# Weaving the attention of each batch by hand into the feed-forward of the batch before it, with 1 KB load runs, 32x32 transposes on VectorE and column-tiled projections

## The chip, the cores and the metric

One core of a Trainium2 chip. The metric is the device time of one execution in microseconds (us). Executions of one kernel agree within about 1%. The profiled span is 1.7 to 1.8 us shorter than the time of the same execution, so sums of profile stretches are compared with spans, and times with times.

Engine names as the profile has them: PE is the matmul side of TensorE, PEld its weight loads, DVE is VectorE, ACT is ScalarE, POOL is GpSimd, SP the engine that only issues transfers here. PSUM is the memory that the matmuls write and the other engines read (the tiles with ps in their names); a copy out of it is an eviction. A column tile is a matmul with 32 weight columns, which fills 32 of the 128 PSUM partitions (`128*32` in the profile). An fp32 matmul shows as two records, which I call passes.

## The reference, cut to what matters

```python
# q, k, v: (4 batches, 4 heads, 1088 tokens, 32), fp32;  S1, S2: (8, 32)
def phi(x):
    a = einsum('rd,bhsd->bhsr', S1, x)
    b = einsum('rd,bhsd->bhsr', S2, x)
    return einsum('bhsi,bhsj->bhsij', a, b).reshape(..., 64)   # outer product
q_p, k_p = phi(q), phi(k)
kv  = einsum('bhsf,bhsd->bhfd', k_p, v)
z   = sum(k_p, over tokens)
att = einsum('bhsf,bhfd->bhsd', q_p, kv) / (einsum('bhsf,bhf->bhs', q_p, z) + 1e-6)
x   = att as (4352 tokens, 128)
out = (maximum(x @ w_gate, 0) * (x @ w_val)) @ w_out           # 128 -> 1536 -> 128
```

The attention needs all keys of a batch before its first query. The feed-forward (FFN) needs only the x of its own tokens. It is worked off in chunks of 512 tokens (8.5 chunks), each with 12 slices of 128 hidden units. I call one slice of one chunk a slot.

## The kernel before

One loop over batches does the attention, 128 tokens at a time. The FFN is a second loop, behind the last batch.

```python
for b in range(B):
    load_qkv(k4, k, nc.sync); load_qkv(q4, q, nc.sync); load_qkv(v4, v, nc.gpsimd)  # 128-byte runs
    for ci in range(NCH):                                    # K half
        nc.tensor.transpose(tr_ps, k4[:, ci], ident)         # fp32, on PE
        nc.vector.tensor_copy(out=tr_sb, in_=tr_ps)
        nc.tensor.matmul(ab_ps, tr_sb, s_bd)                 # 64 projected columns
        nc.scalar.copy(out=ab_sb, in_=ab_ps)
        ...                                                  # zbig, outer product on POOL, kv
    ...
    for ci in range(NCH):                                    # Q half: the same, 96 columns
        ...                                                  # then transposes, num / den, x transposed

for (c0, cs) in TCH:                                         # the FFN
    for j in range(NJ):
        nc.tensor.matmul(g_ps, wg_sb[:, j], xT[:, c0:c0+cs])
        nc.scalar.activation(out=g_sb, in_=g_ps, func=Relu)
        nc.tensor.matmul(v_ps, wv_sb[:, j], xT[:, c0:c0+cs])
        nc.vector.tensor_tensor(out=ht[:, j], in0=g_sb, in1=v_ps, op=mult)
    for j in range(NJ):
        nc.tensor.matmul(ot_ps, wo_sb[:, j], ht[:, j], start=(j==0), stop=(j==NJ-1))
    ...                                                      # transpose back, store
```

A scheduler decides the final order of the instructions on each engine.

Of the kernel before, what the change touches and what calls it, by code (L numbers as in the profile page):

```python
# [8 lines left out]
FP32 = mybir.dt.float32  # L10
BF16 = mybir.dt.bfloat16
FP16 = mybir.dt.float16
ALU = mybir.AluOpType
ACTF = mybir.ActivationFunctionType
XSCALE = 1.0 / 16.0


@with_exitstack
def kernel(
# [12 lines left out]
    nc = tc.nc  # L32
# [5 lines left out]
    NTOK = B * S  # L38
# [4 lines left out]
    SC = 128  # L43
    NCH = (S + SC - 1) // SC
    csz = [min(SC, S - i * SC) for i in range(NCH)]
    NFULL = S // SC
    CLAST = S - NFULL * SC
    HR = H * R

    const = ctx.enter_context(tc.tile_pool(name="const", bufs=1))  # L50
    xpool = ctx.enter_context(tc.tile_pool(name="xpool", bufs=1))
    a_in = ctx.enter_context(tc.tile_pool(name="a_in", bufs=2))
    a_tr = ctx.enter_context(tc.tile_pool(name="a_tr", bufs=5))
    a_ab = ctx.enter_context(tc.tile_pool(name="a_ab", bufs=5))
    a_kp = ctx.enter_context(tc.tile_pool(name="a_kp", bufs=5))
    a_qpt = ctx.enter_context(tc.tile_pool(name="a_qpt", bufs=5))
    a_sm = ctx.enter_context(tc.tile_pool(name="a_sm", bufs=6))
    a_pb = ctx.enter_context(tc.tile_pool(name="a_pb", bufs=2))
    f_h = ctx.enter_context(tc.tile_pool(name="f_h", bufs=2))
    f_g = ctx.enter_context(tc.tile_pool(name="f_g", bufs=4))  # L60
    f_o = ctx.enter_context(tc.tile_pool(name="f_o", bufs=4))


    ident = const.tile([128, 128], FP32)
    make_identity(nc, ident)
    ident16 = const.tile([128, 128], FP16)
    make_identity(nc, ident16)

    s_bd = const.tile([HD, 2 * HR], FP32)
    nc.vector.memset(s_bd, 0.0)  # L70
    for h in range(H):
        nc.scalar.dma_start(out=s_bd[h * D:(h + 1) * D, h * R:(h + 1) * R],
                            in_=S1.transpose([1, 0]))
        nc.scalar.dma_start(out=s_bd[h * D:(h + 1) * D, HR + h * R:HR + (h + 1) * R],
                            in_=S2.transpose([1, 0]))

    s1f = const.tile([HR, HD], FP32)
    nc.vector.memset(s1f, 0.0)
    for h in range(H):
        nc.scalar.dma_start(out=s1f[h * R:(h + 1) * R, h * D:(h + 1) * D], in_=S1)  # L80

    wg_sb = const.tile([DM, NJ, 128], FP16)
    nc.gpsimd.dma_start(out=wg_sb, in_=moe_w_gate.rearrange("m (j f) -> m j f", j=NJ))
    wv_sb = const.tile([DM, NJ, 128], FP16)
    nc.gpsimd.dma_start(out=wv_sb, in_=moe_w_val.rearrange("m (j f) -> m j f", j=NJ))
    wo_sb = const.tile([128, NJ, DM], FP16)
    nc.gpsimd.dma_start(out=wo_sb, in_=moe_w_out.rearrange("(j f) m -> f j m", f=128))

    xT = xpool.tile([HD, NTOK], FP16)

    with tc.tile_pool(name="ps_tr", bufs=2, space=bass.MemoryType.PSUM) as ps_tr, \
         tc.tile_pool(name="ps_xt", bufs=1, space=bass.MemoryType.PSUM) as ps_xt, \
         tc.tile_pool(name="ps_ab", bufs=1, space=bass.MemoryType.PSUM) as ps_ab, \
         tc.tile_pool(name="ps_kv0", bufs=1, space=bass.MemoryType.PSUM) as ps_kv0, \
         tc.tile_pool(name="ps_kv1", bufs=1, space=bass.MemoryType.PSUM) as ps_kv1, \
         tc.tile_pool(name="ps_zb", bufs=1, space=bass.MemoryType.PSUM) as ps_zb, \
         tc.tile_pool(name="ps_nd", bufs=1, space=bass.MemoryType.PSUM) as ps_nd:
        ab2_ps = ps_ab.tile([SC, 2, 96], FP32, name="ab2_ps")
        ndq2_ps = ps_nd.tile([SC, 512], FP32, name="ndq2_ps")
        xtsz_ps = ps_xt.tile([HD, 96], FP32, name="xtsz_ps")  # L100

        for b in range(B):
            q4 = a_in.tile([SC, NCH, H, D], FP32, name="q4")
            k4 = a_in.tile([SC, NCH, H, D], FP32, name="k4")
            v4 = a_in.tile([SC, NCH, H, D], FP16, name="v4")

            def load_qkv(dst, src, eng):
                for h in range(H):
                    eng.dma_start(
                        out=dst[:, 0:NFULL, h],  # L110
                        in_=src[b, h, 0:NFULL * SC, :].rearrange("(c p) d -> p c d", p=SC),
                    )
                eng.dma_start(
                    out=dst[:CLAST, NFULL],
                    in_=src[b, :, NFULL * SC:, :].transpose([1, 0, 2]),
                )

            load_qkv(k4, k, nc.sync)
            load_qkv(q4, q, nc.sync)
            load_qkv(v4, v, nc.gpsimd)  # L120

            kv_ps = [ps_kv0.tile([128, 2 * D], FP32, name="kv0_ps"),
                     ps_kv1.tile([128, 2 * D], FP32, name="kv1_ps")]
            zbig_ps = ps_zb.tile([HR, HR], FP32, name="zbig_ps")
            kv_bd = a_pb.tile([128, 2, F], FP16, name="kv_bd")
            s_bd_ext = a_pb.tile([HD, 3 * HR], FP32, name="s_bd_ext")
            zbig_sb = a_pb.tile([HR, HR], FP32, name="zbig_sb")

            nc.gpsimd.tensor_copy(out=s_bd_ext[:, 0:2 * HR], in_=s_bd)

            for ci in range(NCH):
                c = csz[ci]

                tr_ps = ps_tr.tile([HD, SC], FP32, name="tr_ps")
                nc.tensor.transpose(tr_ps[:, :c], k4[:c, ci].rearrange("s h d -> s (h d)"), ident[:c, :c])  # L135
                tr_sb = a_tr.tile([HD, SC], FP32, name="tr_sb")
                nc.vector.tensor_copy(out=tr_sb[:, :c], in_=tr_ps[:, :c])  # L137

                ab_ps = ab2_ps[:, ci % 2]
                nc.tensor.matmul(ab_ps[:c, 0:2 * HR], tr_sb[:, :c], s_bd, start=True, stop=True)  # L140
                ab_sb = a_ab.tile([SC, 96], FP32, name="ab_sb")
                nc.scalar.copy(out=ab_sb[:c, 0:2 * HR], in_=ab_ps[:c, 0:2 * HR])  # L142

                nc.tensor.matmul(  # L144
                    zbig_ps,
                    ab_sb[:c, 0:HR],
                    ab_sb[:c, HR:2 * HR],
                    start=(ci == 0), stop=(ci == NCH - 1),
                )

                kp = a_kp.tile([SC, H, R, R], FP16, name="kp")
                a_bc = ab_sb[:c, 0:HR].rearrange("s (h i) -> s h i", h=H)[:, :, :, None].to_broadcast([c, H, R, R])
                b_bc = ab_sb[:c, HR:2 * HR].rearrange("s (h j) -> s h j", h=H)[:, :, None, :].to_broadcast([c, H, R, R])
                nc.gpsimd.tensor_tensor(out=kp[:c], in0=a_bc, in1=b_bc, op=ALU.mult)  # L154

                for p in range(2):
                    kp_pair = kp[:c, 2 * p:2 * p + 2].rearrange("s h i j -> s (h i j)")
                    nc.tensor.matmul(  # L158
                        kv_ps[p],
                        kp_pair,  # L160
                        v4[:c, ci, 2 * p:2 * p + 2].rearrange("s h d -> s (h d)"),
                        start=(ci == 0), stop=(ci == NCH - 1),
                    )

            nc.scalar.copy(out=zbig_sb, in_=zbig_ps)
            nc.gpsimd.memset(kv_bd, 0.0)
            for p in range(2):
                nc.scalar.mul(out=kv_bd[0:F, p, 0:D], in_=kv_ps[p][0:F, 0:D], mul=XSCALE)
                nc.scalar.mul(out=kv_bd[F:128, p, D:2 * D], in_=kv_ps[p][F:128, D:2 * D], mul=XSCALE)

            sz_ps = xtsz_ps[:, 64:96]
            nc.tensor.matmul(sz_ps, s1f, zbig_sb, start=True, stop=True)
            nc.gpsimd.memset(s_bd_ext[:, 2 * HR:], 0.0)
            for h in range(H):
                nc.scalar.copy(out=s_bd_ext[h * D:(h + 1) * D, 2 * HR + h * R:2 * HR + (h + 1) * R],  # L175
                               in_=sz_ps[h * D:(h + 1) * D, h * R:(h + 1) * R])

            for ci in range(NCH):
                c = csz[ci]
                s0 = ci * SC  # L180

                tr_ps = ps_tr.tile([HD, SC], FP32, name="tr_ps")
                nc.tensor.transpose(tr_ps[:, :c], q4[:c, ci].rearrange("s h d -> s (h d)"), ident[:c, :c])  # L183
                tr_sb = a_tr.tile([HD, SC], FP32, name="tr_sb")
                nc.scalar.copy(out=tr_sb[:, :c], in_=tr_ps[:, :c])

                ab_ps = ab2_ps[:, ci % 2]
                nc.tensor.matmul(ab_ps[:c], tr_sb[:, :c], s_bd_ext, start=True, stop=True)  # L188
# [120 lines left out]
```

## Time and profile before

| | before |
|---|---|
| time, median of 3 runs | 224.61 us (223.93 to 225.66) |
| profiled span | 223.3 us |
| start of the dense FFN (first value matmul) | 144.18 us; the prediction reads about 143.5 |
| one batch of attention | 29.4 us |
| one FFN chunk | 8.5 us |

The page's first part gives busy time and its share of the span, its second cuts the span in 40 slices (the prediction shows those), and its third counts the packets of the transfers:

```profile
span 223.3 us, 3087 instructions
...
PE 179.1 (80%) x906; PEld 105.7 (47%) x906; DVE 106.2 (48%) x290; ACT 103.2 (46%) x307; POOL 82.1 (37%) x187
...
DMA packets 61776, 9.18 MB, mean 41 GB/s; under 512 B 57152, under 2 KB 61504, under 8 KB 61760
```

PE at 80% looks nearly full, but it is an average over two phases with different limits.

### The profile page before, as it was taken

The page shows a single profiled execution, that of the slowest core. Times are in us where ns is not written, and L with a number is a line of the kernel's source. Part 1 is how long each engine was busy: PE and PEld are TensorE (multiplying, and loading weights), DVE is VectorE, ACT ScalarE, POOL GpSimd, SP SyncE. Part 2 cuts the span into 40 slices and gives each one's busy share as a digit, 9 for nine tenths or more (in the row PEclk, how much of TensorE's full clock was granted, in tenths as well). Part 3 has the DMA queues.
Part 4 walks back from the last instruction along what each step waited for, and adds up shares of the span by engine and source line. Part 5 has one row for each costly group of instructions (what it writes and reads, how often), then busy time and mean ns, then how long its engine had stood idle before and what let it go on. Part 6 is the DMA issues. An engine that isn't in the chain of part 4 may idle for free.

```text
span 223.3 us, 3087 instructions
## 1 busy us (share of the span) xinstructions
PE 179.1 (80%) x906; PEld 105.7 (47%) x906; DVE 106.2 (48%) x290; ACT 103.2 (46%) x307; POOL 82.1 (37%) x187
## 2 busy tenths in 40 slices
PE   0018999659949989689997795599999999999992
PEld 0005666437727667366674552234444444444460
DVE  0002003333114431224422154369998989989981
ACT  0021243112433213332234362158898988988981
POOL 8402578997378853158632385000000000000000
PEclk9999999999999999999999999559999999999998
DMA  7999989765494100000000000000110110110110
GB/s 95 156 125 135 156 107 84 72 23 44 72 52 72 28 0 0 3 0 1 0 1 3 0 0 1 0 0 3 47 48 0 47 51 0 47 42 6 50 47 23
DMA packets 61776, 9.18 MB, mean 41 GB/s; under 512 B 57152, under 2 KB 61504, under 8 KB 61760
## 3 DMA queue, kind: packets, MB, share of 16 engines
q1 hardware_dynamic: 39952, 6.69, 17.8%
q0 software_dynamic: 19568, 2.30, 17.0%
q10 hardware_dynamic: 2240, 0.01, 0.7%
q8 instruction: 7, 0.11, 0.2%
q14 instruction: 9, 0.07, 0.1%
HBM read 9.06 MB, written 2.23 MB: 51 GB/s over the span
## 4 chain that ended last, share of the span: by engine, by line
PE 60%; POOL 18%; DMA 7%; issue 5%; DVE 4%; ACT 4%; SPq 0%; ACTq 0%; POOLq 0%
PE v_ps L255 12%; PE ot_ps L260 10%; PE g_ps L250 10%; POOL qp L195 8%; PE ab_ps L140 7%; DMA k<-in_k_dram 4%; PE zbig_ps L144 4%; POOL den L223 3%; POOL bw L215 3%; PE tr_ps L183 3%; PE kv_ps L158 2%; DMA s_bd<-in_S_dram 2%; PE xtsz_ps L236 2%; PE ndq_ps L211 2%; PE ab_ps L188 2%
## 5 line engine op out<-in xcount | busy, mean ns | idle before, releaser
L256 DVE TENSOR_TENSOR ht<-g_sb,v_ps 128x512 f16<-128x512 f16 (+1 forms) x108 | 67.3, 656 | 8.1 <-PE v_ps L255 4.0
L252 ACT ACTIVATE g_sb<-g_ps 128x512 f16<-128x512 f32 (+1 forms) x108 | 59.1, 583 | 11.5 <-PE g_ps L250 7.9
L255 PE MATMUL v_ps<-xT,wv_sb 128*128 128x512 f16 (+1 forms) x108 | 40.7, 379 | 0.8 <-DVE ht L256 0.4
L250 PE MATMUL g_ps<-xT,wg_sb 128*128 128x512 f16 (+1 forms) x108 | 40.9, 382 | 0.0
L260 PE MATMUL ot_ps<-ht,wo_sb 128*128 128x512 f16 (+1 forms) x108 | 39.8, 374 | 0.2 <-DVE ht L256 0.2
L154 POOL TENSOR_TENSOR kp<-ab_sb 128x256 f16<-128x256 f32 (+1 forms) x36 | 22.2, 623 | 23.8 <-ACT ab_sb L142 20.6
L135 PE MATMUL tr_ps<-ident,k 128*128 128x128 f32 (+1 forms) x36 | 14.7, 435 | 17.8 <-DMA k<-in_k_dram 14.2
L188 PE MATMUL ab_ps<-s_bd_ext,tr_sb 128*128 128x96 f32 (+1 forms) x72 | 25.3, 455 | 4.5 <-ACT s_bd_ext L175 2.6
L195 POOL TENSOR_TENSOR qp<-ab_sb 128x256 f16<-128x256 f32 (+1 forms) x36 | 22.5, 625 | 13.1 <-ACT ab_sb L190 12.3
L142 ACT COPY ab_sb<-ab_ps 128x64 f32<-128x64 f32 (+1 forms) x36 | 7.6, 211 | 41.0 <-PE ab_ps L140 31.8
L140 PE MATMUL ab_ps<-s_bd,tr_sb 128*128 128x64 f32 (+1 forms) x72 | 23.5, 431 | 2.3 <-DMA s_bd<-in_S_dram 2.3
L188 PEld LDWEIGHTS ab_ps<-s_bd_ext,tr_sb 128*128 128x128 f32 (+1 forms) x72 | 17.1, 298 | 9.6 <-ACT ab_sb L190 5.4
L137 DVE COPY tr_sb<-tr_ps 128x128 f32<-128x128 f32 (+1 forms) x36 | 9.6, 275 | 25.4 <-PE tr_ps L135 21.9
L222 DVE TENSOR_REDUCE den<-bw 128x4 f32<-128x32 f32 (+1 forms) x36 | 6.6, 184 | 30.6 <-POOL bw L215 30.3
L190 ACT COPY ab_sb<-ab_ps 128x96 f32<-128x96 f32 (+1 forms) x36 | 8.6, 238 | 25.7 <-PE ab_ps L188 22.4
L140 PEld LDWEIGHTS ab_ps<-s_bd,tr_sb 128*128 128x128 f32 (+1 forms) x72 | 17.5, 305 | 4.7 <-issue 3.1
L208 DVE COPY qpt<-ndq_ps 128x256 f16<-128x256 f16 (+1 forms) x36 | 10.0, 277 | 17.8 <-PE ndq_ps L202 17.2
L135 PEld LDWEIGHTS tr_ps<-ident,k 128*128 128x128 f32 (+1 forms) x36 | 8.0, 229 | 20.9 <-issue 14.4
L250 PEld LDWEIGHTS <-wg_sb 128*128 128x128 f16 x108 | 11.1, 103 | 13.2 <-issue 4.7
L260 PEld LDWEIGHTS <-wo_sb 128*128 128x128 f16 x108 | 10.6, 98 | 14.1 <-issue 3.8
L255 PEld LDWEIGHTS <-wv_sb 128*128 128x128 f16 x108 | 10.7, 99 | 12.6 <-issue 2.9
L237 ACT COPY xT<-xtsz_ps 128x128 f16<-128x128 f16 (+1 forms) x36 | 9.4, 261 | 14.8 <-PE xtsz_ps L236 14.7
(44 smaller groups left out, 207.5 us busy)
## 6 DMA issues: line engine op xcount, KB each, us to landing
k<-in_k_dram SPq DMA_DIRECT2D x16, 128.0 KB, 3.5
q<-in_q_dram SPq DMA_DIRECT2D x16, 128.0 KB, 4.6
out_dram<-o_sb SPq DMA_DIRECT2D x8, 256.0 KB, 2.3
v<-in_v_dram POOLq DMA_DIRECT2D x16, 64.0 KB, 3.4
wg_sb<-in_moe_w_gate_dram POOLq DMA_DIRECT2D x1, 384.0 KB, 5.9
wv_sb<-in_moe_w_val_dram POOLq DMA_DIRECT2D x1, 384.0 KB, 7.5
wo_sb<-in_moe_w_out_dram POOLq DMA_DIRECT2D x1, 384.0 KB, 11.0
s_bd<-in_S_dram ACTq DMA_DIRECT2D x8, 1.0 KB, 5.6
```

What stands on the lines that cost most here:

```text
L135: nc.tensor.transpose(tr_ps[:, :c], k4[:c, ci].rearrange("s h d -> s (h d)"), ident[:c, :c])
L137: nc.vector.tensor_copy(out=tr_sb[:, :c], in_=tr_ps[:, :c])
L140: nc.tensor.matmul(ab_ps[:c, 0:2 * HR], tr_sb[:, :c], s_bd, start=True, stop=True)
L154: nc.gpsimd.tensor_tensor(out=kp[:c], in0=a_bc, in1=b_bc, op=ALU.mult)
L188: nc.tensor.matmul(ab_ps[:c], tr_sb[:, :c], s_bd_ext, start=True, stop=True)
L195: nc.gpsimd.tensor_tensor(out=qp[:c], in0=a_bc, in1=b_bc, op=ALU.mult)
L208: nc.vector.tensor_copy(out=qpt[:, :, :c], in_=qpt_ps[:, :, :c])
L250: nc.tensor.matmul(g_ps[:, :cs], wg_sb[:, j], xT[:, c0:c0 + cs], start=True, stop=True)
L252: nc.scalar.activation(out=g_sb[:, :cs], in_=g_ps[:, :cs], func=ACTF.Relu)
L255: nc.tensor.matmul(v_ps[:, :cs], wv_sb[:, j], xT[:, c0:c0 + cs], start=True, stop=True)
L256: nc.vector.tensor_tensor(out=ht[:, j, :cs], in0=g_sb[:, :cs], in1=v_ps[:, :cs], op=ALU.mult)
L260: nc.tensor.matmul(ot_ps[:, :cs], wo_sb[:, j], ht[:, j, :cs], start=(j == 0), stop=(j == NJ - 1))
```

## The change

Its intent is to fill the half-idle engines of each phase with the work of the other. Batch 0 runs its attention alone. From then on the attention of batch b is issued, slot by slot, between the FFN slots of batch b-1, by an explicit plan and with the scheduler off. K and Q come in 1 KB runs instead of 128-byte ones. Their transposes are 32x32-block transposes on VectorE instead of PE transposes with evictions. The projections use four column tiles of 32 columns each, and q is divided by the denominator before its outer product. The core of the diff, with cuts marked:

```diff
+    if MANUAL:
+        ctx.enter_context(tc.manual_schedule())
 ...
-                    eng.dma_start(out=dst[:, 0:NFULL, h],
-                        in_=src[b, h, 0:NFULL * SC, :].rearrange("(c p) d -> p c d", p=SC))
+            engs[h % len(engs)].dma_start(
+                out=dst[h * D:(h + 1) * D, 0:32].rearrange("t (g c) d -> t g (c d)", g=4),
+                in_=src[b, h, 0:SM, :].rearrange("(g t c) d -> t g (c d)", g=4, t=32))
+        for g in range(2):                                   # the last 64 tokens, 128-byte runs
+            engs[g % len(engs)].dma_start(out=dst[:, 32 + g], in_=src[b, :, SM + 32 * g:SM + 32 * g + 32, :])
 ...
-                nc.tensor.transpose(tr_ps[:, :c], q4[:c, ci].rearrange("s h d -> s (h d)"), ident[:c, :c])
-                nc.scalar.copy(out=tr_sb[:, :c], in_=tr_ps[:, :c])
-                nc.tensor.matmul(ab_ps[:c], tr_sb[:, :c], s_bd_ext, start=True, stop=True)
-                nc.scalar.copy(out=ab_sb[:c], in_=ab_ps[:c])
+        nc.vector.transpose(out=qT[b][:, a * 32:e * 32], in_=q4[b][:, a:e].rearrange("p c d -> p (c d)"))
+        for s in range(3):                                   # sketch 1, sketch 2, denominator
+            for g in range(4):                               # column tile
+                nc.tensor.matmul(ps[32 * g:32 * g + 32, s * 128:(s + 1) * 128],
+                                 s_bd[:, s] if s < 2 else w_s[b], qT[b][:, c_cols(g, 4 * i, 4 * i + 4)])
+        nc.vector.transpose(out=ab[0:n], in_=st["qab", key][0:n, 0:384])
 ...
+    for b in range(1, B):
+        base = 2 * NJ * b                                    # first FFN slot of batch b
+        plan_k(b, base - 25)                                 # all this lies in slots of batch b-1
+        plan_q((b, 0), base - 9)
+        plan_q((b, 1), base - 5)
+    plan_q("rest", 2 * NJ * (B - 1) + 3)                     # the last 64 queries of all batches
+    for n in range(NSLOT):
+        at(n, ffn_gv, n)                                     # gate matmul, ReLU, value matmul of slot n
+        at(n + 0.9, ffn_mul, n)
+        at(n + lag, ffn_out, n)
+    for _, _, fn, a in sorted(table, key=lambda x: x[:2]):
+        fn(*a)
```

## The prediction

> **What bounds the kernel now.** I read the page's slices first, then the table by stage, then the chain, waits and timelines.
>
> ```profile
> PE   0018999659949989689997795599999999999992
> PEld 0005666437727667366674552234444444444460
> DVE  0002003333114431224422154369998989989981
> ACT  0021243112433213332234362158898988988981
> POOL 8402578997378853158632385000000000000000
> PEclk9999999999999999999999999559999999999998
> ```
>
> Two phases, hardly overlapped: POOL, which only attention uses, goes silent where DVE and ACT become full. The table by stretches (us, then busy us of each engine) takes one attention batch and one FFN chunk of 512 tokens:
>
> ```profile
> 79.28:108.64 29.36, 25.63 (x138) 18.12 (x138) 9.32 (x46) 9.29 (x45) 15.31 (x38) 1.00 0.00 1
> 187.50:196.00 8.50, 8.50 (x41) 3.70 (x40) 7.83 (x13) 7.49 (x15) 0.00 (x0) 1.00 0.11 31
> ```
>
> A batch takes 29.4 us (from the K phase of batch 2 to that of batch 3), and in it DVE and ACT are busy 9.3 us each: room for FFN work. An FFN chunk takes 8.5 us with PE, DVE and ACT all nearly full. The FFN starts at about 143.5 us, so 64% of the span is attention. In that phase the chain of waits jumps between engines:
>
> ```profile
> 97.76 0.62 POOL qp L195
> 99.03 0.59 POOL qp L195
> 100.25 0.58 POOL qp L195
> ```
>
> This is the Q half: one outer product each 1.2 us with its small POOL companions between. The first 17 us compute nothing, since K and the 4-byte-run S tables must land:
>
> ```profile
> 1.84 9.90 DMA k<-in_k_dram
> 11.76 5.04 DMA s_bd<-in_S_dram
> ```
>
> For the unit costs I read starts in the timelines, not durations, because matmul durations overlap: first four rows of the cold FFN start, then three of the steady FFN.
>
> ```profile
> 147.20 0.63 PE L260 MATMUL ot_ps<-ht,wo_sb 128*128 128x512 f16 x1
> 147.62 0.63 PE L250 MATMUL g_ps<-xT,wg_sb 128*128 128x512 f16 x1
> ...
> 187.35 0.38 PE L260 MATMUL ot_ps<-ht,wo_sb 128*128 128x512 f16 x1
> 187.56 0.38 PE L255 MATMUL v_ps<-xT,wv_sb 128*128 128x512 f16 x1
> 187.78 0.38 PE L250 MATMUL g_ps<-xT,wg_sb 128*128 128x512 f16 x1
> ```
>
> A 128x512 fp16 matmul costs 0.215 us of PE warm and 0.43 cold. Read alike, smallest start-to-start: the FFN multiply 0.605 us on DVE (256 columns 0.338, so 0.072 + 1.04 ns a column), the ReLU 0.476 on ACT (256: 0.264, so 0.052 + 0.83 ns a column), the POOL outer product of 256 elements 0.57 (of 32: 0.193, so 1.7 ns an element, 1.0 us for 512), an fp16 transpose on PE 0.055.
>
> **What the Trainium skill says.**
> "TensorE: Matmul & The Clock Gate", Part 1: the PE clock is halved until a window of about 3.4 us was busy. The trace agrees: 143.5 to 150.3 us, 6.8 us, ran at 0.5. In attention the record says 1.00, but most fp16 transposes started 0.107 us apart and not 0.055, so I take attention as mostly cold.
> "TensorEngine Tiling (Array Packing)", Key Properties: column tiles work independently, and a change of tiling mode drains the engine. Nothing here uses several column tiles at once. The drain shows: the two passes of the 32-column L144 start 0.075 us apart, the 128-column matmul behind them 0.17 us later.
> "VectorE: DVE Perf Modes", The three transpose paths: DVE transposes only within 32x32 blocks. No row here has one; I take 1 element a cycle like the other DVE work.
> "DMA: Bandwidth & Descriptors", Why small descriptors are slow: a fixed cost per packet. The trace agrees in kind: 57152 of 61776 packets are under 512 B, and loads ran at 125 GB/s in the first 17 us.
>
> **The change part by part.**
> *FFN arithmetic*: unchanged, 8.5 chunks. PE per chunk: 36 x 0.215 + 4 x 0.055 = 7.96 us (8.5 measured, so 6% bubbles).
>
> *Removed*: PE transposes of Q and K and their evictions, the ACT and DVE evictions of the projections, the x transposes; q is divided by the denominator before the outer product, so the numerator comes out transposed already.
>
> *Added on DVE, per batch*: 32x32 transposes of K and Q, 2 x (2 x 384 + 320 columns) = 2.7 us; of the projections 256 + 320 + 2 x 384 columns, 1.7 us; denominators and small copies about 1.2 us. Sum 5.6. Two chunks of FFN are 24 x 0.605 = 14.5, so DVE needs 20.1 us per batch.
>
> *ACT per batch*: 28 x 0.476 for ReLU and outputs, 2 evictions of 1024 columns at 0.90 and 2 of 512: 16.1 us. *POOL*: K 4 x 1.0 + 0.57, Q 4 x 1.0, smaller products about 1.5, DMA issue 1.6: 12 us. Neither bounds.
>
> *PE per batch*: two chunks 15.9 us; 18 kv matmuls at 0.05, 9 zbig at about 0.18 with their mode switches, 16 transposes, 4 x 0.215, sz: 4.7 us together. The disputed term is the fp32 projections: 80 passes of 128 moving columns and 16 of 32. From the cold spacings of the old projections (64 columns 0.268, 96 columns 0.321) a pass streams 1.67 ns a column cold, on top of a weight load that is not hidden; zbig (32 weights, 32 columns, 0.075) leaves 0.022 for a 32-column load. So 128 columns cost about 0.235 cold, 0.118 warm, and the batch 80 x 0.118 + 16 x 0.038 = 10.0 us if tiles do not overlap. With perfect fourfold overlap it would be 2.6, but about 0.046 per pass was the fastest issue seen, so 96 passes cannot go below 4.4. Each fp32 matmul has two passes on the same tile, which must follow each other, so I expect only the second pass of one tile to overlap with the first of the next: about 6.5 us.
> Sum 15.9 + 4.7 + 6.5 = 27.1 us per batch against 20.1 on DVE: PE bounds. But the load is uneven: a slot (1/24 of a batch) with a DVE transpose costs DVE about 1.07 us and PE 0.65, one with a Q projection PE over 2 us. With two PSUM buffers for gate and value only part evens out; taking the larger engine slot by slot gives 32, smoothing gives some back, so 28.
>
> *Prologue.* K goes first in 1 KB runs. Six issues at 0.57 us from 0.7, then a landing: K at about 6.3 us. Then three transposes 1.4, K projections cold 5, their transposes and outer products to about 15.5, kv and z to 18.5, two Q projections cold 3.6 each, outer products, transposes, evictions, numerators; the in-order PE does both halves of batch 0 before the first gate matmul. FFN start at about 30 us, against 143.5.
>
> *End.* The last 2.5 chunks host only the 256 remaining query rows: 2 x 8.5 + 3 + 4.4, then 4.3 us as before from the last ot to the stored result.
>
> *Sum*: 30 + 3 (cold first window or two of the FFN, as in the clock record now) + 3 x 28 + 28.7 = 145.7. I say 145.
>
> **The rivals.**
> A: column tiles overlap almost perfectly. Then a batch needs 15.9 + 4.7 + 4.4 = 25 us of PE, the prologue is some 3 us shorter, and DVE's uneven slots come next: 27 + 2 + 75 + 28.7 = about 133. For: the intent, and the skill; against: two passes on one tile.
> B: no overlap. 30.6 us per batch plus the uneven slots gives 32, the prologue grows by 4: 34 + 3 + 96 + 28.7 = 162. For: in the trace no fp32 weight load hides behind its own matmuls.
> C: woven in-order waits replace the old phase. One late qp or xT on the PE queue holds up gate and value, then DVE and ACT run dry. For: the old chain has many short waits, and the projections, transposes, numerators and outputs share two PSUM buffers. Against: the plan puts one to three slots, about 1 to 3 us, between producer and consumer, and a 512-element POOL product takes 1.0 us in 1.5 slots. If it costs 2 us more per batch: 151.
> D: loads still bound. Late weights would delay the FFN start. Weights, K, Q and V of batch 0 are about 3.8 MB to read, which at 125 to 180 GB/s takes 21 to 30 us; it could bind near 30, but only wo comes late and longer runs help.
>
> **Range and chances.** The main spread is the batch period, 25 to 32 us, counted three times (133 to 162 with the prologue's part); the prologue adds some 4 us either way. So 131 to 161. Even a period of 50 us would only give 211, below the 224.6 now, so slower is very unlikely: faster 0.97, same 0.02, slower 0.01.
>
> **What would show it right or wrong.** Right: POOL busy in tenths until about two thirds of the span; first gate matmul at 26 to 34 us; K landed by 7 us; gate and value spread at 24 slots per 25 to 32 us with PE over 90% and DVE about 70%; granted clock 1.0 after the first FFN microseconds; the last 2.5 chunks at 8.5 us. The start-to-start of the projection passes tells 0.118 (no overlap) from 0.07 (half) and 0.046 (issue-bound). Wrong: DVE above 90% in the woven part (a transpose then costs more than 0.47 us per 384 columns), the chain running through POOL or ACT there, PE at half clock again, or a wait on wg or wv at the FFN start.

## More of the kernel before

The costliest groups carry, after the bar, the engine's idle time just before them and what ended it:

```profile
L256 DVE TENSOR_TENSOR ht<-g_sb,v_ps 128x512 f16<-128x512 f16 (+1 forms) x108 | 67.3, 656 | 8.1 <-PE v_ps L255 4.0
L252 ACT ACTIVATE g_sb<-g_ps 128x512 f16<-128x512 f32 (+1 forms) x108 | 59.1, 583 | 11.5 <-PE g_ps L250 7.9
```

In the FFN before, VectorE and ScalarE hardly wait: 8.1 us of idle for 108 multiplies.

## The result, and the profile after

| | before | after |
|---|---|---|
| time, median of 4 runs | 224.90 us (223.93 to 225.66) | 164.75 us (164.23 to 165.39) |
| profiled span | 223.3 us | 163.4 us |
| packets under 512 B, of all | 57152 of 61776 | 5840 of 13535 |

The ratio is 0.7319 (95% interval 0.7286 to 0.7352). Ratios here are the mean time of one kernel's runs over that of the other's runs of the same rounds, so not quite the ratio of the medians quoted. Executions over 1.5% slower than the fastest of the same kernel are left out of the means. The kernel takes 27% less time, as the direction of the prediction said, and the result is correct. But 164.75 us lies above the range of 131 to 161.

The page of the changed kernel, first and second part and packets:

```profile
span 163.4 us, 2891 instructions
...
PE 122.2 (75%) x1038; PEld 61.1 (37%) x1038; DVE 100.2 (61%) x213; ACT 83.2 (51%) x146; POOL 51.1 (31%) x75
...
PE   0025884579997987779978885999887777999960
...
DVE  4313927415966678548648883786677546788740
...
POOL 8401614601940166156105625240176016000000
```

The phases are gone: POOL works until slice 34 of 40, and DVE is at 3 to 9 tenths beside it. But in the woven middle PE is mostly at 7 to 9 tenths, with one slice at 5, not "over 90%". The table by stages (start:end and length in us, busy us with instruction counts of PE, PEld, DVE, ACT and POOL, then clock, transfer share and GB/s) shows the prologue, the three woven batches, and the tail chunk by chunk:

```profile
0.00:34.66 34.66, 15.10 (x155) 9.65 (x155) 14.41 (x46) 4.10 (x5) 13.32 (x28) 1.00 0.88 148
34.66:63.66 29.00, 26.39 (x222) 12.46 (x221) 20.85 (x42) 16.96 (x29) 11.78 (x15) 1.00 0.12 20
...
94.88:126.10 31.22, 26.57 (x234) 13.05 (x234) 21.41 (x43) 19.00 (x32) 10.73 (x14) 1.00 0.05 17
126.10:141.10 15.00, 11.68 (x112) 5.44 (x112) 8.20 (x16) 9.53 (x17) 3.21 (x5) 1.00 0.05 19
141.10:150.40 9.30, 9.04 (x43) 3.77 (x41) 7.96 (x13) 8.35 (x16) 0.00 (x0) 1.00 0.09 31
```

Three things stand out against the prediction. The FFN starts at 34.66 us, not 30. A woven batch takes 31.22 us, not 28. And a chunk with no attention beside it (141.10 to 150.40) takes 9.30 us, where the kernel before needed 8.5 with the same instructions. No engine is full in a woven batch: DVE is busy 21.4 of 31.2 us, ACT 19.0 and POOL 10.7. PE's busy figure of 26.6 uses modelled ends and counts its pipelined matmuls long.

I put the excess together from the trace, against the predicted sum of 145.7, all in spans. The FFN start is 4.7 us late. From the first value matmul (35.09, 0.4 us after the gate) to the value matmul that opens the last two and a half chunks (126.32) it is 91.2 us, where I had 3 + 3 x 28 = 87, so 4.2 more. The tail from there to 163.43 is 37.1 us instead of 28.7, so 8.4 more. 4.7 + 0.4 + 4.2 + 8.4 = 17.7 us, which is 163.4 less 145.7.

**The prologue.** The chain that ended last, from the start (start us, length us, what):

```profile
2.90 0.74 SPq L82
3.69 9.44 DMA k<-in_k_dram
13.22 0.52 DVE kT L181
...
32.79 1.02 ACT qpt L343
```

The last piece of K is issued at 3.69 us and takes 9.44 us to land, although it has only 16 KB (part of this it stands behind the earlier pieces, for alone with Q and V it took 4.97 us in e2). Where the prediction has K at 6.3 us, the third K transpose starts at 13.22.

**The gate and the value.** In the waits view (what an engine waited for, us in total, times, longest) the two largest that touch the FFN are these:

```profile
ACT g_sb L377 <- PE g_ps L375: 39.4, 57, 2.4
...
DVE ht L386 <- ACT g_sb L377: 35.0, 45, 5.6
```

The multiply waits 35.0 us in 45 waits for the ReLU. In the kernel before, all idle time in front of the multiply was 8.1 us. A timeline of the chunk without attention (start us, length us, engine, line, operation) shows the pattern:

```profile
145.62 1.99 DVE L386 TENSOR_TENSOR ht<-g_sb,v_ps 128x512 f16<-128x512 f16 x3 [0.28 <-PE g_ps L375]
...
145.88 0.38 PE L375 MATMUL g_ps<-xT,wg_sb 128*128 128x512 f16 x1
146.37 0.38 PE L379 MATMUL v_ps<-xT,wv_sb 128*128 128x512 f16 x1
...
146.80 0.38 PE L375 MATMUL g_ps<-xT,wg_sb 128*128 128x512 f16 x1
...
147.21 0.60 ACT L377 ACTIVATE g_sb<-g_ps 128x512 f16<-128x512 f32 x1 [0.32 <-PE g_ps L375]
```

The value matmul at 146.37 starts 0.49 us after its gate, not 0.21, because one of the two value buffers must first be freed by a multiply. The next gate stands behind it in PE's queue, so it starts only at 146.80, and ScalarE then sits idle 0.32 us until it ends. The plan issues gate and value of one slot next to each other. In the order that the scheduler chose for the kernel before, gates ran ahead. Counting gate and value matmuls in its trace, the gate was one or two slots ahead in all but one slot of its second and third chunk, which took 8.10 us each, and from the fourth to the eighth chunk one slot ahead in seven or eight of twelve slots and level in the others, at 8.5 us a chunk. In the changed kernel it is level in all 108.

**The woven waits.** From a timeline in the third batch:

```profile
97.19 1.02 ACT L343 COPY qpt<-ps_a 128x1024 f16<-128x1024 f16 x1
...
98.74 0.69 DVE L386 TENSOR_TENSOR ht<-g_sb,v_ps 128x512 f16<-128x512 f16 x1 [1.14 <-ACT g_sb L377]
...
99.93 0.43 PE L201 MATMUL ps_a<-kT,s_bd 128*32 128x128 f32 x8 [1.08 <-DVE kab L212]
...
101.06 0.60 ACT L377 ACTIVATE g_sb<-g_ps 128x512 f16<-128x512 f32 x1 [2.35 <-PE g_ps L375]
```

A copy of 1.02 us on ACT delays the ReLU behind it, the multiply on DVE waits 1.14 us for that ReLU, the transpose of the projection stands behind the multiply on DVE, and PE waits 1.08 us for that transpose. Meanwhile no gate is issued, and ACT runs dry for 2.35 us. Adding up in the trace, for this batch, every start-to-start gap on PE beyond the usual spacing of its kind gives 7 to 8 us of such stalls. The three largest are 1.25 us before the second K projection, 1.1 before the transposes of the output, and 1.0 in the middle of the first Q projection, whose last third needs the tile w_s (for the denominator), which is not ready.

### The profile page after: what moved, and what is told of

It reads as the page before. It is cut to its first block, busy times and chain, and to the rows that moved or that the text cites. A ratio compares the mean times of both kernels' runs of the same rounds, so it can differ in the third digit from the quotient of the medians.

```text
span 163.4 us, 2891 instructions
## 1 busy us (share of the span) xinstructions
PE 122.2 (75%) x1038; PEld 61.1 (37%) x1038; DVE 100.2 (61%) x213; ACT 83.2 (51%) x146; POOL 51.1 (31%) x75
## 2 busy tenths in 40 slices
DMA packets 13535, 9.20 MB, mean 56 GB/s; under 512 B 5840, under 2 KB 12240, under 8 KB 13520
## 4 chain that ended last, share of the span: by engine, by line
PE 50%; DVE 16%; ACT 12%; DMA 6%; POOL 6%; issue 5%; SPq 2%; POOLq 1%; DVEq 0%; ACTq 0%
PE g_ps L375 11%; PE ot_ps L393 10%; DVE ht L386 10%; PE v_ps L379 9%; DMA k<-in_k_dram 6%; ACT g_sb L377 6%; ACT qpt L343 4%; POOL qp L217 4%; PE kv_ps L242 4%; PE ps_a L201 3%; PE ps_a L337 2%; PE kv_ps L237 2%; ACT xT L362 2%; PE ps_a L358 2%; PE ps_a L285 2%
## 5 line engine op out<-in xcount | busy, mean ns | idle before, releaser
L377 ACT ACTIVATE g_sb<-g_ps 128x512 f16<-128x512 f32 (+1 forms) x108 | 61.7, 575 | 43.4 <-PE g_ps L375 39.4
L217 POOL TENSOR_TENSOR kp<-kab 128x512 f16<-128x512 f32 (+1 forms) x18 | 16.6, 941 | 35.5 <-DVE kab L212 29.1
L343 ACT COPY qpt<-ps_a 128x1024 f16<-128x1024 f16 (+1 forms) x9 | 8.7, 964 | 26.4 <-PE ps_a L337 26.4
L217 POOL TENSOR_TENSOR qp<-a,qab 128x512 f16<-128x512 f32 (+2 forms) x18 | 18.2, 1030 | 6.5 <-DVE a L319 5.2
L201 PE MATMUL ps_a<-kT,s_bd 128*32 128x128 f32 x128 | 9.0, 332 | 15.0 <-DVE kT L181 12.7
L337 PE MATMUL ps_a<-ident,qp 128*128 128x128 f16 (+1 forms) x72 | 10.0, 237 | 5.9 <-POOL qp L217 5.9
L379 PEld LDWEIGHTS <-wv_sb 128*128 128x128 f16 x108 | 10.7, 99 | 9.7 <-issue 2.0
L181 DVE STREAM_TRANSPOSE kT<-k 128x384 f32<-128x384 f32 (+1 forms) x12 | 6.4, 543 | 7.0 <-DMA k<-in_k_dram 7.0
L237 PEld LDWEIGHTS <-kp 128*128 128x128 f16 x72 | 6.4, 100 | 8.6 <-issue 1.8
L242 PE MATMUL kv_ps<-kab 128*32 128x32 f32 x72 | 9.6, 218 | 0.0
L237 PE MATMUL kv_ps<-v,kp 128*128 128x64 f16 x72 | 8.6, 204 | 1.2 <-DVE kp L217 1.2
L188 DVE STREAM_TRANSPOSE qT<-q 128x384 f32<-128x384 f32 (+1 forms) x12 | 6.3, 537 | 0.0
## 6 DMA issues: line engine op xcount, KB each, us to landing
wo_sb<-in_moe_w_out_dram POOLq DMA_DIRECT2D x1, 384.0 KB, 12.6
```

The costliest lines, as they stand in the source:

```text
L201: nc.tensor.matmul(ps[32 * g:32 * g + 32, s * n:s * n + m], s_bd[:, s], kT[b][:, c_cols(g, c0, min(c1, NC))], start=True, stop=True)
L217: eng.tensor_tensor(out=dst.rearrange("p c (h i j) -> p (c h) i j", h=H, i=R), in0=a.rearrange("p c h i -> p (c h) i")[:, :, :, None].to_b ...
L237: nc.tensor.matmul(ps[:, p * 64:(p + 1) * 64].rearrange("p (h d) -> p h d", h=2), st["kp", b, c][:, p * 128:(p + 1) * 128], v4[b][:, 2 * p ...
L242: nc.tensor.matmul(ps[32 * j:32 * j + 32, 128:160], ab[:, 0, o].rearrange("p h r -> p (h r)"), ab[:, 1, o].rearrange("p h r -> p (h r)"), ...
L337: nc.tensor.transpose(st["qpt", key][:, p, c * n:(c + 1) * n], st["qp", key, c][0:n, p * 128:(p + 1) * 128], ident16[0:n, 0:n])
L343: nc.scalar.copy(out=t[:, :, 0:4 * n], in_=st["qpt", key][:, :, 0:4 * n])
```

## The experiments

Theory after reading the result: three separate causes. (1) K's last pieces share the 16 DMA engines with the FFN weights. (2) The value matmul in front of the next gate costs about 0.8 us a chunk. (3) What remains of a woven batch are waits of instructions that stand behind one another in the engines' queues and share two PSUM buffers. Rivals: ScalarE or VectorE simply full; the projections dearer than thought; the loads' run length.

### e1_gate_ahead: the gate one slot ahead of the value

```diff
-        at(n, ffn_gv, n)
+        if n % (2 * NJ) == 0 and n < B * 2 * NJ:
+            at(n - 0.45 if n else n, ffn_g, n)
+        if (n + 1) % (2 * NJ) or n + 1 >= B * 2 * NJ:
+            at(n, ffn_g, n + 1)
+        at(n + 0.01, ffn_v, n)
```

(ffn_gv is split into its gate and value halves; a batch's first gate is pulled ahead by less than half a slot, since its x is only just ready.)

> The only edit: the gate matmul and its ReLU of slot n+1 are issued before the value matmul of slot n, as the kernel before had it in its FFN. Theory (order): in the changed kernel a value buffer is held while ACT still works on the gate of the same slot; by my sum 0.22 + 1.76 us of latency over two buffers gives 0.77 us a slot, the 9.1 us of its chunk 7. With the gate ahead the hold falls to about 1.1 us, chunk 7 comes to 8.0 to 8.5 us, the last chunk loses 1 us, and each woven batch 2 to 4 us because late ACT work no longer stops DVE at once: 150 to 158 us. Rival (other waits decide): the stalls on shared PSUM buffers and on w_s stay as they are, the woven batches stay at 31.2 us, and only the tail gains: 161 to 164 us.

Measured: correct, 157.11 us (156.49 to 157.64), ratio 0.6977 (0.6941 to 0.7013). The third batch, by the table by stages:

```profile
78.37:107.40 29.03, 25.69 (x236) 13.04 (x235) 21.54 (x44) 18.93 (x32) 10.73 (x13) 1.00 0.14 34
```

29.03 us instead of 31.2, with the same instructions. In the waits view the ReLU's wait for the gate falls from 39.4 to 29.6 us, and the multiply now waits for the value matmul instead of the ReLU:

```profile
DVE ht L394 <- PE v_ps L387: 30.0, 39, 5.9
ACT g_sb L377 <- PE g_ps L375: 29.6, 41, 1.6
```

The order costs 7.6 us of the run, or 2.2 us of a batch. K landed 0.7 us later here than in the changed kernel (13.95), so the gain is not from the prologue. About 5 us of stalls per batch remain. (The sum in the expectation is wrong: 0.22 + 1.76 us over two buffers is 0.99 us a slot and not 0.77. The chunk measured 9.30 / 12 = 0.775.)

### e4_ffn_alone and e5_ffn_alone_gate_ahead: the FFN without woven attention

The plans of batches 1 to 3 and of the rest are taken out, and x of batch 0 is copied over the others by POOL, so that the result is wrong. e5 adds the edit of e1 to it.

```diff
-        plan_k(b, base - 25)
-        plan_q((b, 0), base - 9)
-        plan_q((b, 1), base - 5)
+        at(2 * b + 4, lambda b=b: nc.gpsimd.tensor_copy(
+            out=xT[:, b * SM:(b + 1) * SM], in_=xT[:, 0:SM]))
```

> Wrong result on purpose: the attention of batches 1 to 3 is left out and their xT is a copy of batch 0's, so that the FFN slots run with nothing woven in. Order theory: a slot costs 0.76 us even without attention, 9.1 us per chunk, so 18.2 of the 31.2 us per batch, and attention costs 13 us on top; total near 34.9 + 8 x 9.1 + 13 - about 3 of cold clock and loads = 119 to 123 us. Rival (the FFN order is as good as before, only attention's waits cost): 8.0 to 8.5 us per chunk, 112 to 116 us.

> The feed-forward alone as in the run of that name (every chunk 9.30 us, 123.44 us in all), and the gate matmul of each slot issued before the value matmul of the slot before it. Wrong result on purpose, as there. If the order of gate and value is what costs 0.775 us a slot, a chunk falls to 8.0 to 8.5 us (the kernel before took 8.5) and the run to about 114 to 118 us. If VectorE or ScalarE bind the chunk (7.63 and 7.7 us busy of 9.0), or the order is only a matter of the woven attention, the chunk stays at 9.2 to 9.3 and the run at 123.

Measured: 123.44 us (two executions; ratio 0.5482, 0.5446 to 0.5519) and 113.96 us (ratio 0.5069, 0.5057 to 0.5081). One chunk of e4, and one of e5:

```profile
53.00:62.30 9.30, 8.64 (x42) 3.69 (x40) 7.93 (x13) 7.98 (x15) 0.00 (x0) 1.00 0.08 29
```

```profile
51.59:59.73 8.14, 8.14 (x41) 3.75 (x40) 7.68 (x13) 7.84 (x15) 0.00 (x0) 1.00 0.09 33
```

With the gate ahead a chunk takes 8.14 us, with DVE busy 7.68 and ACT 7.84 of it. Without, it takes 9.30, with all engines below 93%. So the order of two matmuls is worth 1.16 us in this chunk (9.5 us over the 8.5 chunks of the two runs, so 1.1 in the mean), and full engines are refuted as the cause of 9.30. The pair gives one more figure: the woven attention adds 31.2 - 2 x 9.30 = 12.6 us to a batch in the changed kernel, and 29.0 - 2 x 8.2 = 12.6 us in e1 (e5's chunks alternate between 8.14 and 8.28). So the cost of the order adds to that of the weaving.

### e2_late_weights: the weights after the last piece of K

```diff
-    wg_sb = ...; nc.gpsimd.dma_start(out=wg_sb, ...)       # likewise wv_sb, wo_sb: moved down
 ...
+    gate = const.tile([128, 2], FP32, name="gate")
+    for g in range(2):                                     # waits for K's last two pieces
+        nc.gpsimd.tensor_copy(out=gate[:, g:g + 1], in_=k4[0][:, 32 + g, 0:1])
+    wg_sb = ...; nc.gpsimd.dma_start(out=wg_sb, ...)       # likewise wv_sb, wo_sb
```

> The only edit: the three weight loads are issued on POOL only after the last piece of K of batch 0 has landed (POOL reads one column of each). Theory (queue sharing): K was late (13.1 us) because its last packets took turns with 3072-byte weight packets on the same 16 DMA engines; K now lands by 6 to 7.5 us, the first projection starts 6 us earlier and the FFN starts at 28 to 30 us: 158 to 160 us. Rival 1 (the 128-byte rest runs or the issue on SP are slow by themselves): K still lands after 10 us and the time stays within 2 us of 164.8. Rival 2 (weights or Q become the new bound): K is early but the FFN starts after 32 us, with a wait on weights or q.

Measured: correct, 160.43 us (159.93 to 160.97), ratio 0.7120 (0.7078 to 0.7163). The chain at the start:

```profile
3.69 4.97 DMA k<-in_k_dram
8.75 0.52 DVE kT L184
```

The same piece, issued at the same moment, lands in 4.97 us instead of 9.44, and the FFN starts at 29.43, which is 5.2 us earlier. That the traffic of the weights held K up is shown, and it costs 4.3 us of the run. The difference to 5.2 is mostly one chunk of the profiled execution, 17.56 us instead of 16.23: between 97.7 and 99.8 us its matmuls start 0.43 us apart instead of 0.215, and the clock record has 0.5 from 96.6 to 100.0. K still landed later than the 6 to 7.5 us that I had expected of this run, so queries and values, which still come beside it, may hold the rest.

### e7_short_runs and e8_short_late: what the 1 KB runs are worth

```diff
-                out=dst[h * D:(h + 1) * D, 0:32].rearrange("t (g c) d -> t g (c d)", g=4),
-                in_=src[b, h, 0:SM, :].rearrange("(g t c) d -> t g (c d)", g=4, t=32),
+                out=dst[h * D:(h + 1) * D, 0:32],
+                in_=src[b, h, 0:SM, :].rearrange("(k t) d -> t k d", t=32),
```

The bytes are the same, the tokens land in another order, so the result is wrong. e8 has the late weights of e2 as well.

> The loads of K and Q in runs of 128 bytes instead of 1024 (the token order is wrong on purpose, so the result is wrong; bytes, instructions and waits stay). If run length is what the early K landing rests on, the eightfold count of packets in K, about 4096 of 13 ns or more on 16 engines, with the weight packets between them, puts the K transpose from 13.2 us to 17 to 25 us and the run to 169 to 177 us; the later batches, whose loads lie under the feed-forward of 30 us, keep their 29 to 31 us. If the weights alone held K back, the K transpose stays near 13 us and the run within 2 us of 164.75.

> Runs of 128 bytes (wrong token order on purpose, so a wrong result) together with the late weights. With the weights early, short runs changed nothing (165.16 against 164.75 us, K transpose 13.12 against 13.22). If the weights hid their cost there, it shows here: K 1.5 to 3 us later than the 8.75 of late weights with long runs, and 161.5 to 163.5 us in all against 160.43. If run length has no part in the landing, K lands near 8.8 us and the run takes 160 to 161.

Measured: e7 165.16 us (164.85 to 165.45), ratio 0.7339 (0.7323 to 0.7355), with 42207 packets instead of 13535. My theory of e7 (169 to 177 us) was wrong. The chain of e7 shows why:

```profile
5.37 7.65 DMA k<-in_k_dram
13.12 0.52 DVE kT L181
```

The third K transpose starts at 13.12, against 13.22 with long runs: the weights set this moment, not the run length. e8 took 161.81 us (161.43 to 162.47), ratio 0.7193 (0.7169 to 0.7217), against 0.7120 for e2. There K is not late (8.29 us), but the last Q transpose starts at 16.84 instead of 15.12, and the FFN at 30.39 instead of 29.43. So my theory of e8 was right in the total and wrong on K: Q pays. The 1 KB runs are worth about 1 to 1.5 us when the weights are out of the way, and nothing measurable in the change as it came.

### e6_tiles_in_turn: is the overlap of the column tiles real?

```diff
-        for s in range(3):
-            for g in range(4):
+        for g in range(4):
+            for s in range(3):
                 nc.tensor.matmul(ps[32 * g:32 * g + 32, s * 128:(s + 1) * 128], ...)
```

(The K projection is changed alike.)

> In the K and Q projections the loops over column tiles and sketches are exchanged, so that the passes of one column tile follow one another and the four tiles come in turn; work, shapes and result stay. If the fourfold overlap comes from neighbours in the stream that lie in different column tiles, it is lost: the starts go from groups of four per 113 ns to one per 60 to 110 ns, the 24 matmuls of a Q projection take 2.5 to 3 us instead of 0.8, a woven batch gets 4 to 7 us longer and the run 15 to 22 us (180 to 187). If TensorE takes matmuls of other tiles out of order, or the projections hide in stalls that are there anyway, the run stays within 2 us of 164.75.

Measured: correct, 172.01 us (171.59 to 172.98), ratio 0.7654 (0.7626 to 0.7682), so 7.3 us slower than the change. First the Q projection of the changed kernel (24 passes in all), then the first four rows of that of e6, from timelines of PE:

```profile
87.86 0.65 PE L285 MATMUL ps_a<-qT,s_bd 128*32 128x128 f32 x16
88.32 0.40 PE L285 MATMUL ps_a<-qT,w_s 128*32 128x128 f32 x8
```

```profile
92.94 0.65 PE L284 MATMUL ps_a<-qT,s_bd 128*32 128x128 f32 x6
93.40 0.27 PE L284 MATMUL ps_a<-qT,w_s 128*32 128x128 f32 x1
93.43 0.30 PE L284 MATMUL ps_a<-qT,s_bd 128*32 128x128 f32 x2
93.51 0.27 PE L284 MATMUL ps_a<-qT,w_s 128*32 128x128 f32 x1
```

In the changed kernel the 24 starts span 0.59 us: four tiles start 7 ns apart, and such groups start 0.10 to 0.13 us after one another. (This is the second Q projection of a batch. The first has 0.99 us more in it, the wait for w_s, and in e6 1.01 us.) In e6 they span 1.31 us. One tile's passes are 0.11 us apart there, so without any overlap 23 steps would take 2.5 us; the next tile's passes do come in early, but the overlap is only about twofold. The mixing shows something more: the program has the w_s passes of the first tile right behind its four s_bd passes, but six s_bd passes start before the first w_s, so a pass of the next tile starts before earlier ones of the tile in front. The overlap is real, and it rests on the order. The loss is half or less of what I expected (15 to 22 us), since the passes of other tiles still mix in.

### e3_q1_later: more slots between the two query chains

```diff
-        plan_q((b, 1), base - 5)
+        plan_q((b, 1), base)
-    plan_q("rest", 2 * NJ * (B - 1) + 3)
+    plan_q("rest", 2 * NJ * (B - 1) + 12)
```

> The only edit: the query plan of the second half of each woven batch is moved 5 slots later (to the batch's own first slot), the remaining rows from slot 3 to slot 12 of the last batch. Theory (two shared PSUM buffers): the worst stalls of a batch, 1.2 us ahead of the second K projection and 1.1 us ahead of the output transposes, come because qpt, num, two kab and ott follow each other in two buffers within four slots. With qpt and num moved away they vanish: 2 us less in each of two batches, 2.5 us less in the chunk behind the third: 157 to 160 us. Rival (ACT's load of 0.9 us evictions in its queue, wherever they stand): the stalls move with the plan and the time stays at 163 to 166 us.

Measured: correct, 162.55 us (162.05 to 163.26), ratio 0.7222 (0.7184 to 0.7259). A batch takes 30.0 us instead of 31.2, and chunk 6 falls to 13.05 us while chunk 7, which now hosts the rest, grows to 11.55. Spreading the chains helps by 2.2 us, less than the theory asked for; most stalls only move.

### c1_combined, c2_two_causes, c3_wider_steps, c4_spread_transposes: do the causes add up, and what is left?

c2 is e1 and e2 together and nothing else. c1 has a wider plan as well:

```diff
-        plan_k(b, base - 25)
-        plan_q((b, 0), base - 9)
-        plan_q((b, 1), base - 5)
+        plan_k(b, base - 27)
+        plan_q((b, 0), base - 10)
+        plan_q((b, 1), base + 2)
```

(c1 also moves the second query half of batch 0 to slot 2 and the rest to chunk 7.) c3 widens the steps inside a query chain too:

```diff
-            at(s + 4.5 + 0.75 * c, q_xpose, key, c)
-        at(s + 7, q_ev, key)
-        at(s + 8, q_num, key)
-        at(s + 8.5, q_x, key)
+            at(s + 5.5 + 0.75 * c, q_xpose, key, c)
+        at(s + 8, q_ev, key)
+        at(s + 9.5, q_num, key)
+        at(s + 9.5, q_x, key)
```

(with plan_k at base - 28, the two query chains at base - 12 and base + 1, the second query half of batch 0 at slot 1, the rest in chunk 7, and the output transpose of a chunk half a slot later). c4 is c3 with the DVE transposes spread, and with the loads of the next batch two slots earlier:

```diff
-            at(s + i, k_transpose, b, i)
+            at(s + i if first else s - 1 + 1.5 * i, k_transpose, b, i)
-                at(s + 6 + i, q_transpose, b, i)
+                at(s + 9 + 1.5 * i, q_transpose, b, i)
```

> Gate matmul ahead (that alone 157.1 us), weights after K (that alone 160.4 us), and the woven attention on wider slots (that alone 162.6 us, of which part was given back in the tail). If the three causes are separate, their gains of 7.6, 4.3 and about 2 us add up and the run takes about 150 to 152 us, with a result that is right and faster than both kernels. If gate ahead and wider slots cure the same stalls, 152 to 155. If K is no longer the first thing that the prologue waits for once the weights come after it, because the weights then land late, 155 or more.

> Gate ahead and late weights, with the plan of the woven attention as in the changed kernel. The run that had both and a wider plan took 153.01 us. If the wider plan gave nothing there, this one takes 152 to 154 us (164.75 less 7.6 less 4.3 is 152.8). If the wider plan is worth the 2 us that it gave alone, it takes 154.5 to 156.

> Gate ahead and late weights, and within each woven query chain the TensorE transposes one slot later, the copy one slot later, the numerator one and a half slots later (the chain starts earlier by as much), so that TensorE finds the GpSimd product and the ScalarE copy ready. In the combined run TensorE lost 5.5 us of a 29.2 us batch, some 2.9 of it in front of these two steps and the gate that waits for the copied numerator. If those waits are what remains, a batch falls to 26.5 to 28 us and the run to 146 to 150. If the waits only move to other places because VectorE and ScalarE work in order and share the slots, it stays at 151 to 154.

> As the run with wider steps (148.79 us), with the woven batches' DVE transposes spread out: K's three 1.5 slots apart from one slot earlier on, Q's three 1.5 slots apart from three slots later on, so that they no longer share their slots with the transposes and denominators of the projections. If the half-microsecond waits between a gate matmul and its value matmul (four of them, about 2.2 us of a batch, in that run) come from DVE work bunched in neighbouring slots, the period of a batch falls from 28.3 us to 26.5 to 27.5 and the run to 145 to 147. If they come from the one transpose before a multiply, wherever it lies, spreading changes nothing: 148 to 149.5.

| kernel | time, us | ratio to before (95%) |
|---|---|---|
| the change | 164.75 (164.23 to 165.39) | 0.7319 (0.7286 to 0.7352) |
| c1_combined | 153.01 (151.60 to 154.04, which is the slow one; the others 151.60 to 153.37) | 0.6782 (0.6744 to 0.6820) |
| c2_two_causes | 151.74 (150.81 to 152.49) | 0.6739 (0.6711 to 0.6767) |
| c3_wider_steps | 148.79 (148.50 to 149.56) | 0.6614 (0.6589 to 0.6638) |
| c4_spread_transposes | 148.44 (148.03 to 148.54) | 0.6598 (0.6580 to 0.6616) |

All four are correct and beat both kernels. c2 is 13.0 us faster than the change, a little more than 7.6 + 4.3 = 11.9: the two causes are separate and add up. The plan of c1 gave nothing on top. c3's longer steps inside a chain, together with its plan, gave 2.9 us beyond c2; no run has the steps alone. Its FFN starts 1.7 us earlier (28.01 instead of 29.73), because the second query half of batch 0 no longer stands before it, but its first batch gives that back: the second batch begins at 57.79 us against 57.37. The gain comes after, 0.7 us in the second batch (28.29 against 29.03) and 2.3 from the third on. So the time came into the expected 146 to 150 us, but the batch period stayed above the expected 26.5 to 28. c4's spreading is not told apart from c3: the expectation of 145 to 147 us was wrong, and bunched transposes are not what is left. Its batch, by the table by stages:

```profile
73.09:101.27 28.18, 26.32 (x235) 13.27 (x234) 22.06 (x43) 18.22 (x32) 10.65 (x13) 1.00 0.05 20
```

DVE is busy 22.1 of 28.2 us, so still no engine is full.

## Why the prediction was right or wrong

The direction was right, and so was its reason: the phases merged, and the FFN starts at 35 us instead of 144. But what bounds a woven batch was wrong. "PE bounds" was the claim, with PE over 90% busy; PE's own work is 23.7 of 31.2 us by the sum below, no engine is full, and waits fill the rest. The time missed by 19.75 us, and these are the steps.

**"Prologue ... K at about 6.3 us": wrong, 4.3 us of the miss.** I reckoned six issues and a landing as if K had the DMA engines to itself. Rival D looked at the weights only as something that the FFN waits for, and added up bytes at 125 to 180 GB/s. What happened is the reverse: the weights came early and held K up. e2 shows it, with the transpose at 8.75 instead of 13.22 us. How they share was not tested. The Trainium skill has in "DMA: Bandwidth & Descriptors", Queues, rings and completion order, that each DMA engine takes turns between its queues, packet by packet. That would fit: in the first 16 us the 3072-byte packets of the gate and value weights took 247 ns each and the 1024-byte packets of K and Q 59 ns (medians), so if a turn is one such packet of each, the weights take the larger part. The rest of the prologue was over-estimated: from the third K transpose to the first gate I had 30 - 6.3 = 23.7 us and it took 21.4.

**"FFN arithmetic: unchanged, 8.5 chunks ... 8.5 measured": wrong, 7.6 us of the miss.** The arithmetic is unchanged, but the 8.5 us belonged to the order of gate and value that the scheduler had chosen (ahead in most slots), and the hand-written plan has another (ahead in none). e4 and e5 show 9.30 and 8.14 us for a chunk, and e1 shows 7.6 us for the whole kernel. I listed the plan's slots and did not ask, for each value matmul, which buffer it waits for and what stands behind it in PE's queue.

**"3 (cold first window or two of the FFN)": too high.** The clock did stay low: at 34.66 us gate and value matmuls start 0.43 us apart, and from 38.1 us on they are near the warm spacing. (The 1.00 in the table by stages does not contradict this: the clock record of this trace begins only at 38.2 us, with 1.0.) But there are no output matmuls in the first slots, which may be why the low clock cost little. The first woven batch took 29.0 us, less than the 31.2 of the later ones, and in e5 the first chunk took 8.38 us against 8.07 to 8.29 for the next seven. My reading of the old clock record was rough as well: it has 0.5 from 139.7 to 149.9 us, not 143.5 to 150.3. FFN matmuls ran at it for 5.7 us there (from 144.18), longer than the window of about 3.4 us that I had cited.

**"Fp32 projections ... about 6.5 us": too high; rival A was right here.** My argument was that two passes of one tile must follow each other and so would block the queue. They do follow each other 0.11 us apart, near my 0.118, but three other tiles run in that time. With 0.59 us for each Q projection (without the wait for w_s) and 0.84 and 0.57 for the two parts of K it is 2.6 us from first to last starts, and with some 0.13 us behind each of the four about 3.1, even below the 4.4 that I had called the issue limit. That limit was wrong too: the fastest issue is 7 ns between tiles.

**"Two PSUM buffers ... only part evens out; ... so 28", and rival C: right kind of cost, far too small.** PE's own work is 15.9 + 4.7 + 3.1 = 23.7 us (the first two as in the prediction, by my estimate there), not 27.1. So uneven slots and in-order waits cost 31.2 - 23.7 = 7.5 us a batch and not 0.9. Of these 2.2 are the order of gate and value (e1). The rest, 5.3, looks in the trace like rival C, for which I had 2, but no run isolated it. The miss of the period, 31.2 against 28, hides two errors against each other: 3.4 us too much for the projections and 6.6 too little for waits. It was a mistake to weigh rival C by the plan's slots between producer and consumer alone: those slots hold a ReLU, a multiply and a copy of 1.0 us that stand in front of other work in the same queues.

**"The last 2.5 chunks host only the 256 remaining query rows: 2 x 8.5 + 3 + 4.4, then 4.3": wrong, 8.4 us, partly the same causes.** The first two chunks took 15.18 and 9.30 us (24.5 instead of 20), for the second query half of batch 3 ends only there, and each chunk has the slow order. The half chunk took 6.8 us from its first value to its last output matmul instead of 4.4. From there to the end it was 5.8 instead of 4.3, of which the trace shows 4.4 after the last instruction on ScalarE, against 2.9 before. The trace has part of the reason: the last rows leave in four stores, two in turn on each of two queues, and their issue ends 1.5 us after that instruction; the kernel before has one store there, issued in 0.4 us. No run tested it.

**The other engines.** DVE's 20.1 us a batch measured 21.4 busy, ACT's 16.1 measured 19.0 (busy durations, which are longer than the start-to-start figures that I used), and POOL's 12 measured 10.7 to 12.1. These sizes held, and the DVE transpose of 384 columns at 0.50 us start to start is near the 0.47 that I had set as a limit.

With the two named causes undone, c2 takes 151.74 us, and with a better plan c4 takes 148.44, 3.4 us above the predicted 145. This does not make the prediction right, for it was of the changed kernel as it came. What stays open are some 4.5 us per batch in c4 (28.2 less 23.7). The trace shows them as a dozen waits of 0.2 to 0.8 us, the longest before a kv matmul (0.8), a value and a gate matmul (0.6 each) and the passes that need w_s (0.4). c1, c3 and c4 moved them more than they removed them. No run isolated one.

## What to carry to other kernels

When a schedule is written by hand, the measured time of an untouched loop is not safe: it belonged to an order, so check for each matmul which buffer it waits for and what it blocks behind it, and issue the producer of the slower chain (here the gate with its ReLU) one step ahead. Large loads that are wanted later can delay what must land first (here by 4.5 us), so try issuing them only once it has landed. Put matmuls of different column tiles next to each other in the stream: here passes of one tile started 0.11 us apart, and those of different tiles 7 ns.

## What the Trainium skill lacked or had wrong

- "TensorE: Matmul & The Clock Gate", Part 3: it has a measured speedup for three column tiles (2.38 times) and for four row tiles (3.07 times), and I did not read it for the prediction. It has none for four column tiles with fp32. Here four tiles start 7 ns apart (it says about 4 ns of issue cost per tile), and 24 passes take 0.59 us start to start where one tile's spacing of 0.11 us would give 2.5.
- "TensorEngine Tiling (Array Packing)", Key Properties: it calls tiles independent, which is right, but does not say that the order in the stream decides. With a tile's passes in a row the 24 took 1.31 us, and the run 7.3 us more.
- "DMA: Bandwidth & Descriptors", Why small descriptors are slow: what it says of a fixed cost is seen (1024 bytes in 51 to 59 ns, 128 bytes in 13, so eight short ones take twice as long). It has no example of how little this can matter: 165.16 us with short runs against 164.75 with long ones. In this kernel the traffic of other loads beside K was worth more (K at 13.2 or 8.75 us).
- "VectorE: DVE Perf Modes", The three transpose paths: its table has a time for 128x128 in bf16 only. Here 128 partitions by 384 columns of fp32, in 32x32 blocks, took 0.56 us (mean of one), and 0.50 from start to start.
- No page that I read treats the order in which two matmuls that feed two other engines go into PE's queue; here it was worth 1.16 us of 9.30 in an FFN chunk.
